# Sink attention and two MoE layers on one core: pinned weight conversions, one joint sink product, and two h groups moved in among the last attention steps

## Chip, cores and metric

The kernel runs on one core of one Trainium2 chip. The metric is the device time of one launch in microseconds (us); the figure used is the median of the runs.

## What is computed

Sliding-window attention with sink keys (2 batches, 8 heads, 768 positions, head dimension 64, 4 sinks, window 128), followed by two feed-forward layers of 1536 tokens, 512 -> 2048 -> 512, with two different activations.

```python
scores = scale * np.matmul(q, k.transpose(0, 1, 3, 2))
keep = is_sink | in_window          # first 4 keys, or the last 128
a = softmax(where(keep, scores, -1e9))
x = np.matmul(a, v)                 # to [1536, 512]
h = x @ w_in
g = where(h >= 1, h, where(h <= -1, 0, (h + 1) ** 2 / 4))
x = g @ w_out
h = x @ w2_in
out = (h * np.clip(h + 3.0, 0.0, 6.0) / 6.0) @ w2_out
```

The four weight matrices arrive as 64-bit floats. The kernel reads them as pairs of 32-bit words (a raw tile of 128 x 512 pairs, 512 KB) and makes 32-bit floats of them on the chip, and from these a high and a low part for the products.

## The kernel before

**Attention.** Two heads form a pair `j`; a pair belongs to one of four groups of query blocks (`GROUPS`, L28), four pairs to a group. Pairs 0 to 3 have four blocks of 128 queries each, pairs 4 to 7 two, pairs 8 to 11 two, pairs 12 to 15 four: 48 units in all. One unit (`j`, `u`) goes through these steps:

- `score` (L300): two fp32 products into `ps_s` (L310), on VectorE mask, scale and row maximum (L317); one step later `expo` (L336, ScalarE, with the row sums), one step later `normalise`: L328 and L329 on VectorE, then two multiplications of `p` on GpSimd (L331).
- `turn` (L357), three units later (`DIST`): TensorE transposes of `p` into `ps_t` (L371, L372) and a copy to `pt` (L353 on ScalarE or L355 on VectorE).
- `sinks` (L377), for units that also see the sinks beside their window: the four sink columns of each head are transposed into `ps_k` (L383, 4 x 128 each) and copied to `pts`.
- `mix` (L386), two steps after a pair's last `turn`: products of `pts` with the sinks' values `vs` and of `pt` with `vraw` into `ps_v` (L408), then `high` and `low` (L134, L136, L141) split the result into `xh` and `xl`.

The order of these steps on TensorE and on SyncE's DMA queue is the program's own (`manual_schedule`, L595). On VectorE, ScalarE and GpSimd the framework orders instructions by a timeline that it simulates while it builds the program: an instruction whose inputs it takes to be ready can come ahead of earlier ones. Each engine then runs its list strictly in order.

**Weights.** `load_w` (L158) loads a raw tile; there are four raw buffers (`RAW`), used in the order 0i0, 0o0, 0i1, 0o1, 0i2, ... (layer, in or out matrix, number). `take` starts a conversion, `narrow` (L168): absolute value (L174 VectorE or L176 ScalarE), clamp (L179), sign (L180), shift and merge (L181) on VectorE, the low word (L184) on ScalarE, and one step later the sum (L186) on VectorE, after which the raw buffer is free. Two steps later `split` makes the high part (L134 or L136) and the low part (L141). The first four raw tiles are loaded halfway through the attention's steps (L604), and 0i0, 0o0, 0i1 are taken 24, 14 and 6 steps before its end (L606 to L611).

**Layers.** For each `fc` (16 of them, a slice of 128 of the 2048 columns), `h_group(m, fc, c)` (L528) does 12 products of 512 columns for a chunk `c` of 512 tokens; `y_group` (L544) 12 more. For c = 0, `activate` follows at once (L511 to L513, then gh and gl by L134, L136, L141), for c = 1, 2 the result is put aside (`hs`, L134). The loop L624 to L636 runs h 0, y of the `fc` before, h 1, h 2 in each round. Tiles of `h` share four PSUM banks with `ps_s`.

## Time and profile before

| | us |
|---|---|
| median of 3 runs | 655.56 (654.04 to 656.28) |
| the profiled execution's own time | 655.16 |
| its span, first to last instruction | 653.40 |
| mean granted TensorE clock | 0.986 |
| TensorE busy | 630.7 (97%) |
| VectorE busy | 423.2 (65%) |
| ScalarE busy | 328.2 (50%) |
| GpSimd busy | 91.5 (14%, all of it in the first 117 us) |

The stages can be told apart by line: L310 to L408 are attention and end at 125.4 us, L534 and L564 are the layers. A busy share over the whole span hides the stages, so the rows further down are cut by stage. "Idle before" is the time an engine stood still before an instruction, and the name behind the arrow is what ended it.

### The profile page before, as it was taken

What the parts mean: (1) busy time and instruction counts of PE and PEld (TensorE: products, weight loads), DVE (VectorE), ACT (ScalarE), POOL (GpSimd) and SP (SyncE); (2) the same over time, 40 slices, a digit from 0 to 9 for tenths busy, and PEclk for the clock granted to TensorE, in tenths of its full rate; (3) what the DMA queues carried; (4) which work ended last, traced back from release to release, by engine and by line L of the source; (5) the groups of instructions that cost most, each with busy time, mean ns of one, the idle gap of its engine ahead of it and who ended that gap; (6) DMA issues with size and microseconds to landing.
All of it is one profiled execution on the core that took longest, in us unless ns stands there. A gap on an engine that the chain in (4) does not pass through costs nothing.

```text
span 653.4 us, 8514 instructions
## 1 busy us (share of the span) xinstructions
PE 630.7 (97%) x3008; PEld 493.6 (76%) x3008; DVE 423.2 (65%) x953; ACT 328.2 (50%) x669; POOL 91.5 (14%) x115
## 2 busy tenths in 40 slices
PE   7997797899999999999999999999999999999997
PEld 4554454588888887888888888888888888888886
DVE  4778888856647567539995597565668302994443
ACT  5777679655455445337663486455533223850001
POOL 7896687200000000000000000000000000000000
PEclk9999799899999999999999999999999999999999
DMA  4237257734453344102223575445451010523203
GB/s 129 88 115 247 70 167 233 229 107 141 129 161 129 115 144 128 65 32 97 98 96 118 174 236 182 162 129 161 129 158 68 34 64 1 192 98 96 97 32 130
DMA packets 32330, 81.38 MB, mean 125 GB/s; under 512 B 3056, under 2 KB 12320, under 8 KB 32288
## 3 DMA queue, kind: packets, MB, share of 16 engines
q1 hardware_dynamic: 32288, 80.84, 38.1%
q8 instruction: 24, 0.39, 0.3%
q14 instruction: 18, 0.15, 0.1%
HBM read 60.91 MB, written 19.92 MB: 124 GB/s over the span
## 4 chain that ended last, share of the span: by engine, by line
PE 72%; DVE 10%; DMA 9%; ACT 6%; issue 2%; POOL 1%; SPq 0%; ACTq 0%; POOLq 0%; DVEq 0%
PE ps_y L564 36%; PE ps_h L534 28%; DMA raw0o<-moe_w_out_dram 6%; PE ps_v L408 3%; PE ps_s L310 3%; DVE w L186 2%; DVE w L181 2%; DMA raw0i<-moe_w_in_dram 2%; ACT p L336 1%; PE ps_t L371 1%; ACT w L176 1%; ACT raw0o L184 1%; DVE w L179 1%; PE ps_t L372 1%; DVE r L512 1%
## 5 line engine op out<-in xcount | busy, mean ns | idle before, releaser
L534 PE MATMUL ps_h<-xh,wi 128*128 128x512 f32 x768 | 242.1, 390 | 0.0
L564 PE MATMUL ps_y<-gh,wo 128*128 128x512 f32 x768 | 241.6, 389 | 0.0
L534 PEld LDWEIGHTS ps_h<-xh,wi 128*128 128x128 f32 x768 | 144.5, 188 | 30.3 <-issue 0.3
L564 PEld LDWEIGHTS ps_y<-gh,wo 128*128 128x128 f32 x768 | 144.1, 188 | 29.9
L564 PE MATMUL ps_y<-gl,wo 128*128 128x512 f32 x384 | 149.6, 390 | 0.6 <-DVE gl L141 0.6
L534 PE MATMUL ps_h<-xl,wi 128*128 128x512 f32 x384 | 149.6, 390 | 0.0
L331 POOL TENSOR_SCALAR p<-p,sm 128x260 f32<-128x260 f32 (+2 forms) x96 | 88.1, 938 | 25.7 <-DVE sm L329 8.6
L564 PEld LDWEIGHTS ps_y<-gl,wo 128*128 128x128 f32 x384 | 72.1, 188 | 16.2 <-DVE gl L141 1.3
L534 PEld LDWEIGHTS ps_h<-xl,wi 128*128 128x128 f32 x384 | 72.2, 188 | 15.0
L179 DVE TENSOR_SCALAR w<-w 128x512 f32<-128x512 f32 x64 | 27.7, 433 | 43.9 <-ACT w L176 42.9
L134 ACT ACTIVATE hs<-ps_h 128x512 f32<-128x512 f32 x64 | 37.5, 589 | 36.4 <-PE ps_h L534 36.3
L336 ACT ACTIVATE p<-p,nm 128x260 f32<-128x260 f32 (+2 forms) x96 | 46.3, 483 | 15.0 <-DVE nm L317 11.4
L141 DVE TENSOR_TENSOR gl<-hs,gh 128x512 fp32r<-128x512 f32 x64 | 44.0, 688 | 12.7 <-ACT gh L134 11.9
L310 PE MATMUL ps_s<-kraw,qraw 64*128 64x260 f32 (+2 forms) x192 | 37.8, 469 | 7.8 <-DMA kraw<-k_dram 4.4
L512 DVE SCALAR_TENSOR_TENSOR r<-r 128x512 f32<-128x512 f32 x48 | 32.3, 685 | 15.6 <-ACT r L511 15.4
L141 DVE TENSOR_TENSOR wi<-w,wi 128x512 fp32r<-128x512 f32 x32 | 22.1, 690 | 30.6 <-ACT wi L134 29.6
L516 DVE SCALAR_TENSOR_TENSOR ps_h<-r,ps_h 128x512 f32<-128x512 f32 x16 | 11.1, 694 | 46.2 <-ACT r L515 46.2
L317 DVE CUSTOM_DVE_ANT_0 p<-ps_s,mask 128x260 f32<-128x260 f32 (+2 forms) x96 | 35.7, 396 | 7.7 <-PE ps_s L310 7.0
L134 ACT ACTIVATE gh<-ps_h 128x512 fp32r<-128x512 f32 x32 | 19.2, 598 | 33.6 <-DVE ps_h L513 21.7
L134 ACT ACTIVATE gh<-hs 128x512 fp32r<-128x512 f32 x35 | 22.0, 629 | 26.0 <-PE ps_y L564 24.8
L572 ACT ACTIVATE o<-ps_y 128x512 f32<-128x512 f32 x6 | 3.6, 596 | 62.5 <-PE ps_y L564 62.5
L136 DVE CAST gh<-hs 128x512 fp32r<-128x512 f32 x29 | 12.3, 426 | 32.8 <-PE ps_y L564 32.7
(72 smaller groups left out, 688.7 us busy)
## 6 DMA issues: line engine op xcount, KB each, us to landing
wo_d<-wo SPq DMA_DIRECT2D x32, 512.0 KB, 5.0
wo<-wo_d SPq DMA_DIRECT2D x32, 512.0 KB, 3.2
raw0i<-moe_w_in_dram SPq DMA_DIRECT2D x16, 512.0 KB, 3.4
raw0o<-moe_w_out_dram SPq DMA_DIRECT2D x16, 512.0 KB, 5.1
raw1i<-moe_w_in_dram SPq DMA_DIRECT2D x16, 512.0 KB, 3.4
raw1o<-moe_w_out_dram SPq DMA_DIRECT2D x16, 512.0 KB, 4.1
out_dram<-o SPq DMA_DIRECT2D x12, 256.0 KB, 2.2
qraw<-q_dram SPq DMA_DIRECT2D x8, 256.0 KB, 2.8
```

The lines of the kernel that those rows point to most:

```text
L134: nc.scalar.activation(out=dst, in_=src, func=AF.Copy)
L141: nc.vector.tensor_tensor(out=dst, in0=src, in1=f32(hi), op=ALU.subtract)
L179: nc.vector.tensor_scalar(out=f32(c), in0=f32(c), scalar1=F64_LOW, scalar2=F64_HIGH, op0=ALU.max, op1=ALU.min)
L181: nc.vector.scalar_tensor_tensor(out=c, in0=c, scalar=3, in1=hi, op0=ALU.logical_shift_left, op1=ALU.bitwise_xor)
L310: nc.tensor.matmul(banks[e], tq[rows, u * P:(u + 1) * P], tk[rows, c0:c0 + w], start=True, stop=True)
L317: nc.vector.tensor_tensor_reduce(out=p[:, e, :], in0=banks[e], in1=masks[min(i, 2)], scale=-SCALE, scalar=BIG, op0=ALU.add, op1=ALU.min, a ...
L331: nc.gpsimd.tensor_scalar_mul(out=p[:, e, :], in0=p[:, e, :], scalar1=sm[:, e:e + 1])
L336: nc.scalar.activation(out=p[:, e, :], in_=p[:, e, :], func=AF.Exp, scale=-1.0, bias=nm[:, e:e + 1], accum_out=sm[:, e:e + 1],)
L408: nc.tensor.matmul(ps[e * D:(e + 1) * D, u0 * P:u1 * P], l, r, start=n == 0, stop=n == len(ops[0]) - 1)
L512: nc.vector.scalar_tensor_tensor(out=r, in0=r, scalar=1.0, in1=r, op0=ALU.min, op1=ALU.mult)
L534: nc.tensor.matmul(ps, w[:, kc, :], x[:, kc, :], start=i == 0, stop=i == len(ops) - 1)
L564: nc.tensor.matmul(ys[dm], a[:, cs], b, start=fc == 0 and i == 0, stop=last and i == 2)
```

## The change

Four edits:

1. The instructions of `narrow` that read the raw tile are pinned behind everything already written for their engine, for the first layer's tiles 0 to 2 of each kind (`keep`).
2. Sinks: after `normalise`, for units with the wide row, a new VectorE instruction scales both heads' sink columns into a tile `psk` of 128 x 8. One transpose of `psk` replaces two of `p`, and one product with eight rows and 128 outputs replaces two with four rows and 64 outputs. `vs` becomes a block-diagonal tile of 8 x 128: GpSimd zeroes it and two DMAs fill it.
3. `h_group(0, 0, 0)` and `h_group(0, 0, 1)` are issued from the attention's steps, five and two steps before the last.
4. The tile that takes the second of these results lies in a pool of its own, opened before the attention.

```diff
+    hs0_p = ctx.enter_context(tc.tile_pool(name="hs0", bufs=1))
...
-    def narrow(t, dst):
+    def narrow(t, dst, keep):
+
+        def place(ins):
+            if keep:
+                tc.keep_in_program_order(ins)
...
-            nc.vector.tensor_scalar(out=c, in0=hi, scalar1=0x7FFFFFFF, scalar2=None, op0=ALU.bitwise_and)
+            place(nc.vector.tensor_scalar(out=c, in0=hi, scalar1=0x7FFFFFFF, scalar2=None, op0=ALU.bitwise_and))
         else:
-            nc.scalar.activation(out=f32(c), in_=f32(hi), func=AF.Abs)
+            place(nc.scalar.activation(out=f32(c), in_=f32(hi), func=AF.Abs))
...
-        nc.vector.tensor_scalar(out=hi, in0=hi, scalar1=-(1 << 31), scalar2=None, op0=ALU.bitwise_and)
+        place(nc.vector.tensor_scalar(out=hi, in0=hi, scalar1=-(1 << 31), scalar2=None, op0=ALU.bitwise_and))
...
-        nc.scalar.activation(out=f32(lo), in_=lo.bitcast(U32), func=AF.Copy, scale=2.0 ** -51, bias=2.0)
+        place(nc.scalar.activation(out=f32(lo), in_=lo.bitcast(U32), func=AF.Copy, scale=2.0 ** -51, bias=2.0))
...
-            narrow(t, t32)
+            narrow(t, t32, m == 0 and fc < 3)
...
-                ts = at_p.tile([NS, P], F32, tag="vs", name="vs")
-                nc.sync.dma_start(out=ts, in_=v[b, 0:NS, cs])
+                ts = at_p.tile([2 * NS, P], F32, tag="vs", name="vs")
+                nc.gpsimd.memset(ts, 0.0)
+                for e in range(2):
+                    ds = slice(e * D, (e + 1) * D)
+                    nc.sync.dma_start(out=ts[e * NS:(e + 1) * NS, ds], in_=v[b, 0:NS, cs][:, ds])
...
+                if w > 2 * P:
+                    ps = at_p.tile([P, 2, NS], F32, tag="psk", name="psk", bufs=DIST + 3)
+                    nc.vector.tensor_tensor(
+                        out=ps, in0=p[:, :, P:KB], in1=sm.unsqueeze(2).to_broadcast([P, 2, NS]), op=ALU.mult
+                    )
+                    psink[j, u] = ps.rearrange("p e s -> p (e s)")
                 for e in range(2):
                     nc.gpsimd.tensor_scalar_mul(out=p[:, e, :], in0=p[:, e, :], scalar1=sm[:, e:e + 1])
...
-                p = probs.pop((j, u))
-                for e in range(2):
-                    nc.tensor.transpose(ps[0:NS, e, n, :], p[:, e, P:KB], ident)
-            copy(pt[j][1][:, :, us[0]:us[-1] + 1, :], ps[0:NS, :, :len(us), :], 2 * len(us) * P)
+                nc.tensor.transpose(ps[0:2 * NS, n, :], psink.pop((j, u)), ident)
+            copy(pt[j][1][:, us[0]:us[-1] + 1, :], ps[0:2 * NS, :len(us), :], len(us) * P)
...
+            sink = us < nq
+            if sink:
+                nc.tensor.matmul(
+                    ps[:, us * P:nq * P], ts, tsink[:, us:nq, :].rearrange("p n q -> p (n q)"), start=True, stop=False
+                )
...
-                if us < nq:
-                    ops[e].append((us, nq, ts[:, cs], tsink[:, e].rearrange("p n q -> p (n q)")[:, us * P:nq * P]))
...
-            t = hs_p[0].tile([P, N], F32, tag=f"h{c}_{fc}", name=f"hs{c}")
+            t = (hs0_p if (c, fc) == (1, 0) else hs_p[0]).tile([P, N], F32, tag=f"h{c}_{fc}", name=f"hs{c}")
...
+                    if n == len(steps) - 5:
+                        h_group(0, 0, 0)
+                        early.append((0, 0, 0))
+                    if n == len(steps) - 2:
+                        h_group(0, 0, 1)
+                        early.append((0, 0, 1))
...
-                h_group(m, fc, 0)
+                if (m, fc, 0) not in early:
+                    h_group(m, fc, 0)
...
-                h_group(m, fc, 1)
+                if (m, fc, 1) not in early:
+                    h_group(m, fc, 1)
```

How the change moves instructions, at three places. In a row stand the line, the operation, what it writes `<-` what it reads (with the buffer's number), the shape of the output, and how often.

ScalarE before, while pairs 12 and 13 pass (L336 the exponentials of a unit, L353 the copies of transposes, L176, L184 and L134 a conversion):

```order
L353 ACTIVATE pts_1288<-ps_k_1341 4x2x256
L176 ACTIVATE w32_1682<-raw0i2_1394 128x512
L184 ACTIVATE raw0i2_1394<-raw0i2_1394 128x512
L336 ACTIVATE p_1351,sm_1353<-p_1351,nm_1352 128x260 x2
L353 ACTIVATE pt_1287<-ps_t_1388 128x2x256
L336 ACTIVATE p_1380,sm_1382<-p_1380,nm_1381 128x260
L353 ACTIVATE pts_1288<-ps_k_1401 4x2x256
```

ScalarE now, from the unit p_1395 of pair 14 on (L350 is the exponential, L367 the copy, L189 the low word, L135 the high part):

```order
L350 ACTIVATE p_1395,sm_1397<-p_1395,nm_1396 128x260 x2
L189 ACTIVATE raw0i0_943<-raw0i0_943 128x512
L367 ACTIVATE pt_1328<-ps_t_1434 128x2x256
L350 ACTIVATE p_1426,sm_1428<-p_1426,nm_1427 128x260
L367 ACTIVATE pts_1329<-ps_k_1449 8x256
L350 ACTIVATE p_1426,sm_1428<-p_1426,nm_1427 128x260
L350 ACTIVATE p_1457,sm_1459<-p_1457,nm_1458 128x260 x2
L367 ACTIVATE pt_1464<-ps_t_1466 128x2x256
L135 ACTIVATE wi0_1408<-w32_1409 128x512
```

Before, the conversion of the fifth raw tile (0i2) stood among the units of pair 13, and those of the first four far ahead of it; now the first raw tile (0i0) is converted there. Counted over ScalarE's list, 14 conversions stood ahead of the first layer's first activation before; now there are 3.

TensorE before, from the mix of pair 14 to the first h group (ps_t turns, ps_k sinks, ps_v mix, ps_h an h group):

```order
L408 MATMUL ps_v_1560<-pt_1418,vraw_1323 64x128 x2
...
L383 MATMUL ps_k_1589<-ident_114,p_1434 4x128 x2
L383 MATMUL ps_k_1589<-ident_114,p_1480 4x128 x2
L371 MATMUL ps_t_1596<-ident_114,p_1510 128x128
...
L383 MATMUL ps_k_1611<-ident_114,p_1540 4x128 x2
L408 MATMUL ps_v_1617<-pts_1549,vs_1456 64x512 x2
...
L534 MATMUL ps_h_1636<-xh0_0_363,wi0_1364 128x512
```

TensorE now:

```order
L421 MATMUL ps_v_1613<-pt_1464,vraw_1365 64x128 x2
...
L393 MATMUL ps_k_1641<-ident_117,psk_1511 8x128
L393 MATMUL ps_k_1641<-ident_117,psk_1553 8x128
L547 MATMUL ps_h_1645<-xh0_0_377,wi0_1408 128x512
...
L385 MATMUL ps_t_1667<-ident_117,p_1561 128x128
...
L547 MATMUL ps_h_1686<-xh0_1_803,wi0_1408 128x512
...
L405 MATMUL ps_v_1701<-pts_1600,vs_1503 128x512
...
L547 MATMUL ps_h_1735<-xh0_2_1371,wi0_1408 128x512
```

The h groups of chunks 0 and 1 now stand between the last turns, and the h group of chunk 2, which reads the result of the last mix, follows that mix directly.

ScalarE at the same place, before (p_1540 is the last unit, ps_v_1560 the mix of pair 14):

```order
L176 ACTIVATE w32_1824<-raw0o3_1703 128x512
L184 ACTIVATE raw0o3_1703<-raw0o3_1703 128x512
L336 ACTIVATE p_1540,sm_1542<-p_1540,nm_1541 128x260 x2
L184 ACTIVATE raw0i4_1705<-raw0i4_1705 128x512
L184 ACTIVATE raw0o4_1754<-raw0o4_1754 128x512
L176 ACTIVATE w32_1864<-raw0i4_1705 128x512
L134 ACTIVATE wi0_1775<-w32_1776 128x512
L134 ACTIVATE wo0_1823<-w32_1824 128x512
L134 ACTIVATE xh0_2_1327<-ps_v_1560 128x512
```

and now (ps_v_1701 is the last mix, L524 the activation of the h group that came early, gh its high part):

```order
L189 ACTIVATE raw0i1_947<-raw0i1_947 128x512
L367 ACTIVATE pts_1600<-ps_k_1641 8x256
L524 ACTIVATE r_1658<-ps_h_1645,half_116 128x512
...
L135 ACTIVATE wi0_1633<-w32_1634 128x512
L367 ACTIVATE pt_1599<-ps_t_1676 128x2x256
L367 ACTIVATE pts_1600<-ps_k_1682 8x256
L135 ACTIVATE gh_1659<-ps_h_1645 128x512
L189 ACTIVATE raw0i3_1673<-raw0i3_1673 128x512
L135 ACTIVATE hs1_1699<-ps_h_1686 128x512
L135 ACTIVATE xh0_2_1371<-ps_v_1701 128x512
```

Tile 0i3 is not among the pinned ones: its L189 stands ahead of the eviction of the last mix. On SyncE's queue its load keeps its place, and it takes the raw buffer that 0i1 leaves.

## Rows read from the trace of the kernel before

**Rows 1.** Engine busy by stage; columns after the stretch: its length, busy PE, PEld, DVE, ACT, POOL, granted clock, DMA.

```profile
59.77:84.20 24.43, 17.17 (x92) 9.06 (x90) 22.20 (x83) 17.06 (x53) 16.04 (x16) 0.79 0.41 139
84.20:92.87 8.67, 8.67 (x67) 4.97 (x65) 6.66 (x32) 7.47 (x25) 7.97 (x9) 1.00 0.59 192
92.87:101.96 9.09, 9.09 (x66) 5.25 (x65) 8.10 (x30) 8.10 (x24) 4.95 (x6) 1.00 0.32 99
101.96:114.93 12.97, 9.68 (x62) 5.00 (x61) 11.38 (x36) 11.98 (x31) 11.02 (x12) 0.92 0.89 302
114.93:125.36 10.43, 7.20 (x46) 4.33 (x44) 8.63 (x17) 7.84 (x15) 2.81 (x2) 0.83 0.85 234
125.36:653.40 528.04, 523.57 (x2306) 432.62 (x2304) 325.36 (x566) 234.80 (x394) 0.00 (x0) 1.00 0.36 117
```

**Rows 2.** TensorE's timeline, 60 to 126 us: start, length, idle before.

```profile
64.79 0.56 PE L310 MATMUL ps_s<-kraw,qraw 64*128 64x128 f32 x4 [3.37 <-DVE sm L328]
...
73.67 0.33 PE L371 MATMUL ps_t<-ident,p 128*128 128x128 f32 x1 [2.82 <-POOL p L331]
...
111.06 1.07 PE L408 MATMUL ps_v<-pts,vs 4*64 4x512 f32 x4 [2.44 <-ACT pts L353]
```

**Rows 3.** SyncE's queue: the first raw load and the key load behind four of them.

```profile
55.46 0.47 SPq L162 DMA_DIRECT2D raw0i<-moe_w_in_dram  x1
...
57.90 0.44 SPq L281 DMA_DIRECT2D kraw<-k_dram  x1
```

**Rows 4.** DMA issues, 57.8 to 58 us: that key load, us to landing.

```profile
kraw<-k_dram SPq DMA_DIRECT2D x1, 128.0 KB, 6.8
```

**Rows 5.** Engine busy, as rows 1, from the key load's landing on.

```profile
64.80:69.30 4.50, 4.50 (x22) 2.56 (x22) 4.35 (x14) 3.27 (x11) 2.41 (x2) 0.62 0.13 43
69.30:73.60 4.30, 1.56 (x13) 0.79 (x12) 4.30 (x18) 3.07 (x12) 0.90 (x2) 1.00 0.78 242
73.60:82.20 8.60, 7.45 (x31) 3.59 (x31) 6.70 (x25) 4.54 (x14) 8.24 (x10) 0.60 0.02 4
```

**Rows 6.** TensorE's timeline, pair 13: sinks, the next score, and a mix's two parts.

```profile
96.25 0.60 PE L383 MATMUL ps_k<-ident,p 128*4 128x128 f32 x4
96.78 0.71 PE L310 MATMUL ps_s<-kraw,qraw 64*128 64x260 f32 x4
...
99.07 1.07 PE L408 MATMUL ps_v<-pts,vs 4*64 4x512 f32 x4
100.08 1.95 PE L408 MATMUL ps_v<-pt,vraw 128*64 128x128 f32 x20
```

**Rows 7.** GpSimd's timeline: a memset, and eight multiplications in one run.

```profile
0.86 0.20 POOL L249 MEMSET mask<- 128x128 f32 x1
...
88.56 7.32 POOL L331 TENSOR_SCALAR p<-p,sm 128x260 f32<-128x260 f32 x8 [0.17 <-ACT p L336]
```

**Rows 8.** Groups by shape, attention: the nearest small VectorE instruction; columns busy us, mean ns.

```profile
L329 DVE RECIPROCAL sm<-sm 128x2 f32<-128x2 f32 x48 | 7.8, 162 | 1.0
```

**Rows 9.** The same view, VectorE, 125 to 246 us: two passes of a conversion, and the activation.

```profile
L179 DVE TENSOR_SCALAR w<-w 128x512 f32<-128x512 f32 x20 | 8.5, 427 | 22.6 <-ACT w L176 22.0
L512 DVE SCALAR_TENSOR_TENSOR r<-r 128x512 f32<-128x512 f32 x11 | 7.6, 688 | 5.1 <-ACT r L511 5.0
...
L186 DVE CUSTOM_DVE_ANT_0 w<-raw0o,w 128x1024 uint16<-128x1024 uint16 x10 | 6.9, 692 | 0.3
```

**Rows 10.** The chain that ended last, first layer: start and length of loads on it.

```profile
144.20 4.30 DMA raw0o<-moe_w_out_dram
...
190.51 4.22 DMA raw0o<-moe_w_out_dram
202.80 4.31 DMA raw0o<-moe_w_out_dram
...
236.87 4.08 DMA raw1o<-moe_w_out_dram
...
298.64 89.76 PE ps_y L564 x396
```

More of the change, by code (lines that the diff above doesn't have):

```diff
@@ L262, in build_fast_attention @@
             at[ci] = col0[-1] + nq * P
-        qk, vv, probs, pt = {}, {}, {}, {}
+        qk, vv, probs, psink, pt = {}, {}, {}, {}, {}
         def geom(gi):
@@ L362, in turn @@
                     at_p.tile([P, 2, NQ, 2, P], F32, tag="pt", name="pt", bufs=2),
-                    at_p.tile([NS, 2, NQ, P], F32, tag="pts", name="pts", bufs=2),
+                    at_p.tile([2 * NS, NQ, P], F32, tag="pts", name="pts", bufs=2),
                 )
-            p = probs[j, u]
+            p = probs.pop((j, u))
             w = widths[min(i, 2)]
@@ L373, in turn @@
             copy(pt[j][0][:, :, u, lo:, :], ps[:, :, lo:, :], 2 * (2 - lo) * P)
-            if i < 2:
-                probs.pop((j, u))
         def sinks(j, us):
-            ps = bank("ps_k").rearrange("p (e u q) -> p e u q", e=2, u=2)
+            ps = bank("ps_k").rearrange("p (u q) -> p u q", q=P)
             for n, u in enumerate(us):
-                p = probs.pop((j, u))
-                for e in range(2):
-                    nc.tensor.transpose(ps[0:NS, e, n, :], p[:, e, P:KB], ident)
-            copy(pt[j][1][:, :, us[0]:us[-1] + 1, :], ps[0:NS, :, :len(us), :], 2 * len(us) * P)
+                nc.tensor.transpose(ps[0:2 * NS, n, :], psink.pop((j, u)), ident)
+            copy(pt[j][1][:, us[0]:us[-1] + 1, :], ps[0:2 * NS, :len(us), :], len(us) * P)
         def mix(j):
@@ L408, in mix @@
                     nc.tensor.matmul(
-                        ps[e * D:(e + 1) * D, u0 * P:u1 * P], l, r, start=n == 0, stop=n == len(ops[0]) - 1
+                        ps[e * D:(e + 1) * D, u0 * P:u1 * P], l, r, start=n == 0 and not sink, stop=n == len(ops[0]) - 1
                     )
@@ L594, in sink_attention_moe_moe_kernel @@
     hs_p = []
+    early = []
     with tc.manual_schedule(engines={mybir.EngineType.PE, mybir.EngineType.SP}):
```

## The prediction

> **What bounds the kernel now.** I read the stages first [rows 1]. From 125.36 us on, the two layers are TensorE's: 523.57 of 528.04 us busy at full clock, and 396 products on the ending chain take 89.76 us [rows 10], 0.2267 us each, or 10.88 us for a round of 48. Nothing in the change removes a layer product, so what can be gained lies before 125.36 us. There the stretches cut at the ends of mixes 7, 11, 12, 13, 14 and 15 differ widely. While pair 12 passes, without a conversion beside it, TensorE is busy for all of 8.67 us and GpSimd for 7.97. Pairs 8 to 11, whose units are narrower, take 24.43 us with TensorE busy for 17.17, at a clock of 0.79. Pair 14 takes 12.97, busy for 9.68. The last turns and the last mix take 10.43, busy for 7.20 at 0.83.
>
> The idle gaps on TensorE [rows 2] name GpSimd's multiplications and ScalarE's copies. These are late because conversions stand in front of them on VectorE and ScalarE: VectorE is busy for 22.20 of the 24.43 us, against 6.66 of 8.67 beside pair 12. One gap is of another kind. The product at 64.79 is said to wait for VectorE, but it is the first score of pair 11, and that pair's keys were asked for at 57.90, behind four raw tiles asked for from 55.46 on [rows 3], and took 6.8 us [rows 4]: they land at 64.7. This wait is a transfer's, and the change leaves the order of those loads alone.
>
> **The sum.** The profiled execution took 655.16 us: 653.40 of span and 1.76 around it. That is 0.4 below the median of 655.56, and 0.3% (2 us) is about what a measurement of this kernel can tell from no change.
>
> *Sinks (A).* Four sink transposes take 0.53 us until the next score starts [rows 6]; two remain, 0.26 less in each of 16 calls: 4.2. Four sink records of 512 columns take 1.01 us until the mix goes on [rows 6]; two remain, 0.50 less in each of four mixes and half of that in the eight with 256 columns: 4.0. So TensorE has 8.2 us less to do. The copies to pts halve their columns, which I leave uncounted. Against it: 32 new small instructions on VectorE, each standing between the reciprocal and GpSimd, since GpSimd overwrites what they read. The trace has none; the nearest row is the reciprocal, 0.16 us [rows 8], together 5.2. And 12 memsets on GpSimd, at most 0.20 each by the wider one [rows 7], 2.4. GpSimd needs 7.32 us for a pair's eight multiplications without a pause [rows 7], so a pair of 8.67 us could not fall below some 7.5. The bounds are a gain of 8.2 (TensorE alone decides) and a loss of 7.6 (GpSimd alone decides and takes all additions). I take a gain of 4.5, a little over half, since beside pair 12 TensorE was the one without a pause and GpSimd had 8% left. The 12 extra DMAs for `vs` are of 1 KB, asked for two pairs ahead; SyncE's queue waits there for a buffer anyway, so I cost them at nothing; if that cover goes, the load behind them is the next pair's keys.
>
> *Conversions beside pairs 8 to 11 (B).* The orders show the first four conversions leave this stretch. After the keys' landing, from 64.80 to 82.20 us, TensorE is busy for 4.50 us at a clock of 0.62, 1.56 at 1.00 and 7.45 at 0.60 [rows 5]: 2.8 + 1.6 + 4.5 = 8.9 us of work at full speed in 17.4. The 3.37 us wait remains, and the low clock behind it, which cost 4.5 - 2.8 = 1.7. So 17.4 becomes 10.6 at best, a gain of 6.8; since three units' latency between score and turn may show where units are narrow, I take 6.0, with bounds of 3 and 6.8.
>
> *Pair 14 (C).* By ScalarE's order one conversion remains beside it, 0o0, and one (0i0) between pairs 13 and 14, where several stood. Beside pair 13 a conversion left the pair at 9.09 us. So 12.97 becomes 9.09, a gain of 3.9 (bounds 2 and 4.3, which is pair 12's 8.67).
>
> *The end (D).* Of the last 10.43 us, 7.20 at 0.83 are work, 6.0 at full speed. The waits for the last units' GpSimd and copies, 4.4 us with the clock's loss, get two h groups put into them, 2 x 12 x 0.2267 = 5.4 us, which the layers then do not have to do. They need xh of chunks 0 and 1, finished long before, and the weights of 0i0, converted some 20 steps earlier. I take all 4.4; the lower bound is 2, if the units' own chain to the last turn shows.
>
> *The first layer (E).* This is what the change pays with. Fourteen conversions stood ahead of the first activation, three do now, so in the first five rounds VectorE has to do about three a round, not two. One conversion is two passes like L179's 0.43 and three like L186's 0.69 [rows 9], 2.9 us; the activation's three passes, like L512's, are 2.1. Three conversions and one activation come to 10.8 us in a round of 10.88: it fits, with nothing over. And where before the h result of chunk 2 had two h groups between itself and the last mix, ScalarE now meets the low word of 0i3 ahead of that mix's eviction. That load starts when 0i1's sum is done. Mix 14's eviction (two passes) and 0i1's conversion follow mix 14 on VectorE, so that is some 4.3 us behind its end; with 4.3 to land [rows 10] ScalarE can go on some 8.7 us behind it, and the last mix ends at about 9.5. So the eviction is hardly late. I take a loss of 2.0 for both; the bounds are 0 and, from the load pace below, 10.5.
>
> Sum: 655.16 - 4.5 - 6.0 - 3.9 - 4.4 + 2.0 = **638.4 us**, rounded to 638, a gain of 17.
>
> **The rivals.**
>
> *GpSimd takes the sinks' gain.* For it: 92% busy beside pair 12 and a new instruction in front of it. Against: the additions are small. A becomes 0, the time 643. Chance 0.11.
>
> *The joint product saves nothing.* If the two heads' sink products ran side by side in the array, on different columns, one product would take as long as two. The row says otherwise: four records 1.01 us apart in all, 0.25 each, about the 0.21 that 512 columns take at 2.4 GHz, so one after the other [rows 6]. A falls by the mixes' half, to 2.3, the time to 641. Chance 0.04. The Trainium skill has the rule in "TensorE: Matmul & The Clock Gate", Part 3: Packing small matmuls: products with outputs on different column tiles run concurrently; by it the mixes would gain nothing. The trace does not agree here.
>
> *The layers lose their lead.* Before, loads of out tiles followed each other from 144.20 to 236.87 us eight times, 11.58 us apart [rows 10], slower than TensorE's 10.88; the lead in converted tiles hid it. Without that lead each of 15 rounds may cost 0.70: E becomes 10.5, the time 647. Against: a conversion's work fits the round, and early on loads are not what ScalarE's list is waiting for. Chance 0.17.
>
> *Slower.* The same place, worse: ScalarE stands in order behind each load, with gh and hs behind it, and every round takes as long as the longest gap, 190.51 to 202.80, 12.29 us [rows 10]. Fifteen rounds cost 21.2, the time 657.6. It decides from 12.2 us a round on, where 15 x 1.3 takes up the gains of 18.8. Against: the mean of the eight gaps is 11.58. Chance 0.04.
>
> *It only moves the waits.* ScalarE and VectorE may be just as late elsewhere, because the same conversions now crowd the last pairs; then B, C and D go and 653 remains at best. Only three of fourteen are left there. Chance 0.03.
>
> **How the numbers follow.** The forecast has the rest, 0.61. The range: all gains at their upper bounds and E at 0 give 655.2 - 8.2 - 6.8 - 4.3 - 4.4 = 631.5, and a keys' wait that shrinks from its 3.37 would take a little more: 629. Upward it takes in the first three rivals with a margin of some 3 us for gains that come short as well: 650. Faster by over 0.3%: 0.61 + 0.11 + 0.04 + 0.17 = 0.93; within it 0.03; slower 0.04.
>
> **What would show it.** Attention (scores, turns, mixes) ends with an h group between turns, and the last mix ends near 110 us, of which 5.4 are h groups; the gap of some 3 us in front of pair 11's first score stays, and the clock falls behind it. VectorE's busy share in pairs 8 to 11 falls clearly below 91%. Between the last two mixes TensorE has no gap over 1 us. Sink records in a mix: two, not four, in half the time. In the first layer, TensorE's gaps add up to about 2 us, named after gl, gh or wi. I am wrong if pairs 8 to 11 still take over 20 us, if GpSimd's pauses grow in pairs 12 to 15, or if gaps of the first layer sum to over 6 us.

## The result, and the profile after

| | before | after |
|---|---|---|
| median of the runs, us | 655.07 (654.04 to 656.28) | 639.95 (638.06 to 640.95) |
| the profiled execution's own time | 655.16 | 638.06 |
| its span | 653.40 | 636.30 |
| TensorE records | 3008 | 2952 |

The ratio is 0.9765, with a 95% interval of 0.9736 to 0.9795: faster, by some 15 us. The prediction was 638 in 629 to 650. So the total and the sign were right. Of the five terms behind them three were near, and two were wrong in opposite directions. A record is one entry of the profile; an fp32 product of the attention shows as two, a transpose as one. The profiled execution is the fastest of the four, with a mean granted clock of 1.000 where the other three had 0.990 to 0.994, so the rows below show some 2 us more gain than the medians.

Here is the windows view of the changed kernel, cut as [rows 1] at the ends of mixes 7, 11, 12, 13, 14 and 15. The columns are the same: length, busy PE, PEld, DVE, ACT, POOL, granted clock, DMA.

```profile
59.25:76.27 17.02, 12.57 (x93) 7.13 (x91) 10.33 (x56) 9.96 (x36) 11.45 (x14) 1.00 0.62 204
76.27:85.98 9.71, 8.96 (x60) 4.68 (x58) 7.95 (x41) 6.81 (x25) 9.23 (x11) 1.00 0.46 144
85.98:94.84 8.86, 8.67 (x60) 5.02 (x58) 7.92 (x37) 8.15 (x27) 5.42 (x7) 1.00 0.02 5
94.84:104.84 10.00, 8.51 (x56) 4.36 (x54) 9.18 (x33) 7.85 (x24) 9.54 (x12) 1.00 0.54 180
104.84:115.21 10.37, 10.37 (x65) 7.57 (x63) 6.30 (x10) 6.09 (x12) 2.83 (x3) 1.00 0.18 60
115.21:636.30 521.09, 517.11 (x2282) 427.85 (x2280) 339.78 (x601) 245.75 (x414) 0.00 (x0) 1.00 0.39 128
```

Beside [rows 1], stage by stage. The two early h groups (5.44 us of work) now lie in the last units; the fifth column takes them out there and puts them into the layers, so that like stands beside like.

| stretch | before | after | difference | with the h groups put back |
|---|---|---|---|---|
| start to mix 7 | 59.77 | 59.25 | -0.5 | -0.5 |
| pairs 8 to 11 | 24.43 | 17.02 | -7.4 | -7.4 |
| pair 12 | 8.67 | 9.71 | +1.0 | +1.0 |
| pair 13 | 9.09 | 8.86 | -0.2 | -0.2 |
| pair 14 | 12.97 | 10.00 | -3.0 | -3.0 |
| last turns, last mix | 10.43 | 10.37 | -0.1 | -5.5 |
| layers | 528.04 | 521.09 | -7.0 | -1.5 |
| span | 653.40 | 636.30 | -17.1 | -17.1 |

VectorE is busy for 10.33 of 17.02 us in pairs 8 to 11, 61% where it was 91%: the conversions have left. In pair 12 GpSimd is now the fullest engine, 9.23 of 9.71, while TensorE stands still for 0.75: that pair has become slower. GpSimd's own pauses did not grow there: from pair 12 to the last mix they sum to 4.4 us, where they were 6.8. Between the last two mixes TensorE has no pause.

TensorE's timeline of the changed kernel, five places: start, length, and in brackets the idle time before and what ended it.

```profile
64.03 0.49 PE L318 MATMUL ps_s<-kraw,qraw 64*128 64x128 f32 x4 [3.12 <-DMA kraw<-k_dram]
64.45 0.87 PE L421 MATMUL ps_v<-pt,vraw 128*64 128x256 f32 x8
...
82.41 0.71 PE L318 MATMUL ps_s<-kraw,qraw 64*128 64x260 f32 x4
83.05 1.12 PE L405 MATMUL ps_v<-pts,vs 8*128 8x512 f32 x2
84.10 1.95 PE L421 MATMUL ps_v<-pt,vraw 128*64 128x128 f32 x20
...
105.47 0.48 PE L547 MATMUL ps_h<-xh,wi 128*128 128x512 f32 x1
...
109.33 0.48 PE L547 MATMUL ps_h<-xh,wi 128*128 128x512 f32 x1
...
112.28 1.12 PE L405 MATMUL ps_v<-pts,vs 8*128 8x512 f32 x2
```

Three things are to be seen. The wait for pair 11's keys stayed, and the trace now names the transfer (before, it named VectorE, [rows 2]); but behind it the clock did not fall in this execution. The one sink product of pair 12 takes from 83.05 to 84.10, 1.05 us, for two records: the four before took 1.01 [rows 6], where the prediction wanted half the time. And the h groups stand at 105.5 and 109.3, among the last units.

### The profile page after: what moved, and what is told of

Its sections match the earlier page's. It is cut to its first block, busy times and chain, and to the rows that moved or that the text cites. A ratio compares the mean times of both kernels' runs of the same rounds, so it can differ in the third digit from the quotient of the medians.

```text
span 636.3 us, 8483 instructions
## 1 busy us (share of the span) xinstructions
PE 619.3 (97%) x2952; PEld 487.8 (77%) x2952; DVE 424.1 (67%) x985; ACT 324.5 (51%) x669; POOL 88.9 (14%) x127
## 4 chain that ended last, share of the span: by engine, by line
PE 89%; DVE 5%; ACT 3%; DMA 2%; issue 1%; POOL 1%; SPq 0%; DVEq 0%; ACTq 0%
PE ps_h L547 41%; PE ps_y L577 41%; ACT p L350 2%; PE ps_s L318 2%; PE ps_v L421 2%; DMA kraw<-k_dram 2%; DVE p L325 1%; PE ps_t L385 1%; PE ps_t L386 1%; PE ps_v L405 1%; POOL p L345 1%; DVE sm L336 1%; DVE pt L369 0%; DVE xl L142 0%; DVE sm L337 0%
## 5 line engine op out<-in xcount | busy, mean ns | idle before, releaser
L345 POOL TENSOR_SCALAR p<-p,sm 128x260 f32<-128x260 f32 (+2 forms) x96 | 83.8, 887 | 17.9 <-DVE sm L337 7.1
L350 ACT ACTIVATE p<-p,nm 128x260 f32<-128x260 f32 (+2 forms) x96 | 46.4, 484 | 27.4 <-DVE nm L325 19.4
L135 ACT ACTIVATE hs<-ps_h 128x512 f32<-128x512 f32 x64 | 37.5, 589 | 37.7 <-PE ps_h L547 36.0
L184 DVE TENSOR_SCALAR w<-w 128x512 f32<-128x512 f32 x64 | 27.4, 428 | 34.0 <-ACT w L181 33.4
L318 PE MATMUL ps_s<-kraw,qraw 64*128 64x260 f32 (+2 forms) x192 | 35.7, 447 | 7.5 <-DMA kraw<-k_dram 7.5
L525 DVE SCALAR_TENSOR_TENSOR r<-r 128x512 f32<-128x512 f32 x48 | 32.3, 686 | 12.3 <-ACT r L524 12.2
L135 ACT ACTIVATE gh<-hs 128x512 fp32r<-128x512 f32 x35 | 22.0, 630 | 25.9 <-PE ps_y L577 24.7
L135 ACT ACTIVATE gh<-ps_h 128x512 fp32r<-128x512 f32 x32 | 19.1, 597 | 25.2 <-DVE ps_h L526 12.9
```

The costliest lines, as they stand in the source:

```text
L135: nc.scalar.activation(out=dst, in_=src, func=AF.Copy)
L184: nc.vector.tensor_scalar(out=f32(c), in0=f32(c), scalar1=F64_LOW, scalar2=F64_HIGH, op0=ALU.max, op1=ALU.min)
L318: nc.tensor.matmul(banks[e], tq[rows, u * P:(u + 1) * P], tk[rows, c0:c0 + w], start=True, stop=True)
L345: nc.gpsimd.tensor_scalar_mul(out=p[:, e, :], in0=p[:, e, :], scalar1=sm[:, e:e + 1])
L350: nc.scalar.activation(out=p[:, e, :], in_=p[:, e, :], func=AF.Exp, scale=-1.0, bias=nm[:, e:e + 1], accum_out=sm[:, e:e + 1],)
L525: nc.vector.scalar_tensor_tensor(out=r, in0=r, scalar=1.0, in1=r, op0=ALU.min, op1=ALU.mult)
```

## The experiments

My theory after the result: the pins and the early h groups carry the gain, the first layer pays nothing, and the sinks edit nets to about nothing, because the two heads' products had run side by side and because GpSimd, not TensorE, sets the pace where the units are wide. The rivals are the terms as predicted, and those named in each expectation.

**1. The pins alone.** Edit 1 on the kernel before.

```diff
-            narrow(t, t32)
+            narrow(t, t32, m == 0 and fc < 3)
```

> The kernel before with the pinned conversion steps alone. My theory: pairs 8 to 11 give some 7 us and pair 14 some 3 by this edit alone, and the first layer loses nothing by the conversions that come to it: 655 - 10 = 645 us (643 to 647), pairs 8 to 11 (end of mix 7 to end of mix 11) in about 17 us. Rival 1, the layers lose their lead and only the two early h groups hid that: 648 or more, with gaps on TensorE in the first rounds. Rival 2, the pins only move the waits: 653 or more.

648.09 us (ratio 0.9900, 0.9879 to 0.9920), by the ratio a gain of 6.6 and not of 10 (in experiments 1 to 4 gains and losses against the kernel before go by the ratio). Windows of this kernel: pairs 8 to 11, 12, 14, and the end.

```profile
58.50:77.75 19.25, 16.57 (x92) 9.13 (x91) 11.03 (x54) 10.55 (x36) 12.09 (x15) 0.73 0.52 177
77.75:89.40 11.65, 10.38 (x66) 5.66 (x65) 7.24 (x35) 7.67 (x25) 10.54 (x13) 0.86 0.46 146
...
98.17:106.94 8.77, 8.42 (x63) 4.64 (x61) 7.77 (x29) 7.31 (x22) 7.25 (x8) 1.00 0.51 180
106.94:118.89 11.95, 8.64 (x47) 4.21 (x45) 4.18 (x6) 5.47 (x10) 3.92 (x5) 0.78 0.20 67
```

The mix of pair 12 on TensorE:

```profile
84.98 1.07 PE L412 MATMUL ps_v<-pts,vs 4*64 4x512 f32 x4 [1.27 <-DVE pts L359]
85.99 3.48 PE L412 MATMUL ps_v<-pt,vraw 128*64 128x128 f32 x20
```

Pairs 8 to 11 give 5.2 (24.43 to 19.25) and pair 14 gives 4.2 (12.97 to 8.77); the end takes 1.5 longer (11.95 where it took 10.43, at a clock of 0.78). But pair 12 goes from 8.67 to 11.65, with GpSimd busy for 10.54 of it. Of these 3.0 us, 1.3 are a wait of the mix for `pts`, copies of transposes of what GpSimd multiplied, and 1.5 are the clock: it fell in that mix, whose 20 records take 3.41 us until the pair ends at 89.40, where the kernel before took 1.89 (90.98 to 92.87). Over the two stretches together GpSimd has much the same to do (24.0 us before, 22.6 here): beside slow narrow pairs the multiplications of the wide units that follow were hidden; once those pairs are quick, they show (my reading; experiment 8 moves a part of them). The layers lost nothing: 527.51 us against 528.04, though here no h group runs early. So rival 1 of the expectation has its time, 648 or more, but not its reason: the layers did not lose their lead.

**2. The sinks edit alone.** Edit 2 on the kernel before.

> The kernel before with the sinks edit alone. My theory since the result: the joint product takes as long as the two it stands for, the transposes save about 0.2 us a call, and the small products on VectorE and GpSimd's memsets take that back: 654 to 656, no change. Rival 1, the term as predicted, 4.5 us: 650.6. Rival 2, GpSimd is held up behind the small products on VectorE: 657 or more, with GpSimd's waits for them over 3 us in all.

656.71 us (ratio 1.0033, 1.0018 to 1.0047): 2.2 us slower by the ratio, 1.1 by the medians. TensorE's waits by releaser, from mix 7 to 126 us, in this kernel (total, times, longest):

```profile
PE ps_v L400 <- ACT pts L362: 6.1, 3, 4.2
PE ps_s L313 <- DVE raw0o L180: 2.9, 1, 2.9
PE ps_t L380 <- POOL p L340: 1.0, 3, 0.5
```

The same view of the kernel before:

```profile
PE ps_v L408 <- ACT pts L353: 4.2, 2, 2.4
PE ps_t L371 <- POOL p L331: 4.2, 4, 2.8
```

The waits for GpSimd fall by 3.2 us, those for the copies of `pts`, which stand behind conversions on ScalarE, grow by 1.9. The predicted 4.5 us are not there. By stage the attention ends 1.2 us earlier (124.16 where it was 125.36), and the layers take 2.6 longer (530.64 where they took 528.04, with TensorE idle for 5.99 against 4.47), which none of the expectations named. Rival 2 has its sign, since GpSimd waits 4.2 us in all for `psk`, and 0.3 us are missing to its 657; but TensorE's waits for GpSimd became shorter, and those that grew are the copies'. So in this kernel rival 2 is neither shown nor excluded.

**3. The early h groups alone.** Edits 3 and 4 on the kernel before.

> The kernel before with the two early h groups alone (and the tile of their own that they need). My theory: the two groups (5.4 us) go into gaps of the last units, which are there with or without the pins: 655 - 4.5 = 650.6 (649 to 652). Rival, the gaps are there but VectorE and ScalarE, with the first conversions unpinned, put the groups' evictions in front of the last units' work: 653 to 656.

653.13 us (ratio 0.9962, 0.9944 to 0.9981), a gain of 2.5, between the gains of the two expectations (3 to 6 us, and 2 at most). Windows of pair 14, the end, and the layers:

```profile
100.52:114.43 13.91, 10.40 (x63) 5.46 (x61) 11.58 (x37) 12.47 (x32) 11.95 (x12) 0.88 0.86 295
114.43:125.18 10.75, 10.75 (x70) 7.80 (x68) 10.67 (x21) 9.32 (x18) 1.87 (x2) 1.00 0.66 196
125.18:649.80 524.62, 519.16 (x2282) 427.23 (x2280) 322.55 (x562) 232.00 (x390) 0.00 (x0) 1.00 0.36 118
```

Less their 5.44 the last units take 5.31 where they took 10.43: a gain of 5.1 in their place, by the mechanism of term D. Without the pins it is given back in part: pair 14 takes 13.91 (12.97 before), and the layers with the groups' 5.44 come to 530.06 (528.04 before), with TensorE idle for 5.46 there against 4.47.

**4. Pins and early h groups, without the sinks edit.**

> The changed kernel without the sinks edit: pins and early h groups. My theory: as fast as the changed kernel, 639 to 641, since the sinks edit is worth nothing. Rival 1, the sinks edit is worth the predicted 4.5: 644.5. Rival 2, it costs, by GpSimd's waits: 636 to 638, with pair 12 back at 8.7 us from 9.7.

642.00 us (ratio 0.9814, 0.9789 to 0.9839): 12.2 us less than before, where the pins alone and the h groups alone give 6.6 + 2.5 = 9.1. They help each other by some 3 us: the end, 11.95 with the pins alone, takes 10.75 with 5.44 of h groups in it. 642 lies between the expectations for the sinks edit's worth, so this kernel and the changed one ran once more, on the same chip:

> The changed kernel once more, on the same chip as the kernel without the sinks edit, for the difference of the two: 640 (639 to 641). Its clock behind the keys' wait should in most executions be below 1.00, unlike in the first profile.

> The kernel without the sinks edit once more, beside the changed kernel on the same chip. If the edit nets to about nothing, as with the raw tiles apart: within 1 us of the changed kernel. If it is worth what the first pair of runs showed: 642, 2 us above it.

640.84 with the sinks edit (ratio 0.9784, 0.9757 to 0.9810), 642.66 without (0.9818, 0.9787 to 0.9848): 1.8 us, near the second expectation, though the intervals overlap. The two profiled executions (640.82 and 644.54) differ by more: by 2.2 us in pairs 8 to 11, which use no sinks and where the granted clock was 0.90 with the edit and 0.74 without, by 1.9 in pair 12 (9.72 and 11.57), and by 1.3 the other way in pair 14 (9.99 and 8.74). The first profiles of the two kernels are alike in pairs 8 to 11 (17.02 and 16.90) and differ by 2.5 in pair 12 (9.71 and 12.23). So pair 12 is where the edit gains. TensorE and GpSimd there in the kernel without the edit:

```profile
86.59 1.07 PE L413 MATMUL ps_v<-pts,vs 4*64 4x512 f32 x4 [1.28 <-DVE pts L360]
87.59 3.38 PE L413 MATMUL ps_v<-pt,vraw 128*64 128x128 f32 x20
```

```profile
77.77 6.40 POOL L336 TENSOR_SCALAR p<-p,sm 128x260 f32<-128x260 f32 x7
84.35 3.67 POOL L336 TENSOR_SCALAR p<-p,sm 128x260 f32<-128x260 f32 x4 [0.17 <-DVE sm L334]
```

GpSimd multiplies for 10 us with one pause of 0.17, and the mix waits 1.28 us for `pts`, a copy of transposes of what GpSimd multiplied (1.27 in this kernel's first profile, and 1.27 with the pins alone). Behind the wait the clock fell here as in experiment 1 (0.87 over the pair, 1.00 with the edit): the mix's 20 records take 3.32 us until the pair ends at 90.91, those of the changed kernel 1.88 (84.10 to 85.98). With the edit the mix at 83.05 above has no wait: `psk` comes from VectorE, so the sinks no longer queue behind GpSimd. That this short cut, and the clock that it kept, is the edit's one real gain is my reading of these rows; no experiment isolates it, and the same wait does not always cost the clock: in experiment 7 without the edit the mix waits 1.34 us, and the clock of the pair is 1.00.

The changed kernel's second profile shows the clock behind the keys' wait as expected, below 1.00, and the mean clocks of all five executions are 0.991 to 0.997:

```profile
59.74:77.56 17.82, 13.97 (x92) 7.88 (x90) 10.42 (x56) 9.96 (x36) 11.45 (x14) 0.90 0.62 200
```

```profile
64.26 0.80 PE L318 MATMUL ps_s<-kraw,qraw 64*128 64x128 f32 x4 [2.86 <-DMA kraw<-k_dram]
64.99 1.55 PE L421 MATMUL ps_v<-pt,vraw 128*64 128x256 f32 x8
```

The same mix that took 0.87 us at 64.45 in the first profile takes 1.55 here, behind a wait of 2.86 us.

**5. The joint product as two of 64 columns.** The changed kernel with one product for each head, both on the 8 rows.

```diff
-                nc.tensor.matmul(
-                    ps[:, us * P:nq * P], ts, tsink[:, us:nq, :].rearrange("p n q -> p (n q)"), start=True, stop=False
-                )
+                for e in range(2):
+                    cs = slice(e * D, (e + 1) * D)
+                    nc.tensor.matmul(
+                        ps[cs, us * P:nq * P], ts[:, cs], tsink[:, us:nq, :].rearrange("p n q -> p (n q)"),
+                        start=True, stop=False,
+                    )
```

> The changed kernel, its one sink product of 128 output columns written as two of 64, one for each head, with the same right-hand side of 8 rows: four records a mix where there are two. If products on different output columns run side by side in the array (my theory now): the four records of pair 12 take the same 1.05 us until the mix goes on, and the time is that of the changed kernel, 639 to 641. If they run one after the other (what the prediction assumed): 2.1 us, 1.05 more in each of four mixes and some 0.6 in each of eight, up to 9 us more, 645 to 649.

640.65 us (ratio 0.9764, 0.9735 to 0.9793), the changed kernel's own ratio. TensorE's timeline, pair 12:

```profile
87.18 1.07 PE L407 MATMUL ps_v<-pts,vs 8*64 8x512 f32 x4
88.18 1.95 PE L424 MATMUL ps_v<-pt,vraw 128*64 128x128 f32 x20
```

Four records of 64 output columns take 1.00 us, two of 128 take 1.05. One after the other they would have taken 2.1. So the heads' products do run side by side, and joining them saves nothing. The single records say it too: of the four, two and two start 7 ns apart, here and in the kernel before (99.074 and 99.081, 99.554 and 99.561 us), while the two of the joint product start 0.53 us apart. That a record of fewer output columns is simply quicker does not fit: the transposes onto 4 columns [rows 6] and those onto 128 before them take 0.27 us each at full clock. By the Trainium skill ("TensorE: Matmul & The Clock Gate", Part 3: Packing small matmuls) products on different column tiles run concurrently; this run agrees, 1.00 us against 1.05, and the prediction's reading of the trace before was wrong.

**6. GpSimd leaves the sink columns alone.** The changed kernel; GpSimd multiplies two blocks of 128 columns, so that it need not wait for VectorE to read the four between them.

```diff
-            p = at_p.tile([P, 2, KB + P], F32, tag="p", name="p", bufs=DIST + 3)[:, :, :w]
+            pw = at_p.tile([P, 2, 2 * KB], F32, tag="p", name="p", bufs=DIST + 3)
+            p = pw[:, :, :w]
...
-                    nc.gpsimd.tensor_scalar_mul(out=p[:, e, :], in0=p[:, e, :], scalar1=sm[:, e:e + 1])
+                    x = p[:, e, :]
+                    if w > 2 * P:
+                        x = pw[:, e, :].rearrange("p (n c) -> p n c", c=KB)[:, :, 0:P]
+                    nc.gpsimd.tensor_scalar_mul(out=x, in0=x, scalar1=sm[:, e:e + 1])
```

> The changed kernel with GpSimd's multiplications leaving out the sink columns of p (two blocks of 128 columns, which nothing else needs the sink columns of), so that GpSimd no longer overwrites what VectorE's small product reads and need not wait for it. If that order is what the sinks edit costs: from the end of mix 0 to the end of mix 7 0.9 us less (40.08 to 39.2), pairs 12 and 14 together 2 us less: 637. If it is the small products' own time on VectorE, or GpSimd's multiplications: 639 to 641, with GpSimd as busy in pair 12 as before. Two blocks may also cost GpSimd more than one: 642 or more.

639.28 us (ratio 0.9750, 0.9726 to 0.9775): no change that can be told, the second expectation. GpSimd's waits, 19 to 106 us, first in the changed kernel, then here:

```profile
POOL p L345 <- DVE sm L337: 4.0, 5, 1.8
POOL p L345 <- DVE sm L336: 3.9, 2, 3.3
POOL p L345 <- DVE psk L340: 3.4, 7, 1.2
```

```profile
POOL p L349 <- DVE sm L338: 8.0, 8, 2.9
...
POOL p L349 <- DVE psk L341: 0.9, 1, 0.9
```

The wait for `psk` falls from 3.4 to 0.9 us and another takes its place. From the end of mix 0 to the end of mix 7 the 0.8 us that the first expectation wanted did come (40.08 to 39.29), though other kernels with the edit lie between 38.76 and 40.08 there; of its 2 us in pairs 12 and 14 only 0.2 came (19.71 to 19.52). So in the wide pairs at the end, standing behind VectorE's small product is not what costs GpSimd its time.

**7. The first raw tiles apart**, with and without the sinks edit. One raw tile every ten steps, so that the keys are not behind four of them.

```diff
-    def load_weights():
-        while issued[0] < min(taken[0] + RAW, len(queue)):
+    def load_weights(most=RAW):
+        end = issued[0] + most
+        while issued[0] < min(end, taken[0] + RAW, len(queue)):
...
-                    if n == len(steps) // 2:
-                        load_weights()
+                    if n - len(steps) // 2 in (0, 10, 20, 30):
+                        load_weights(1)
```

> The changed kernel with the first four raw weight tiles asked for one at a time, ten steps apart, and not all four ahead of pair 11's keys. If the keys' wait of 3.1 us is a transfer's that ends the line of work there: it shrinks below 1 us, pairs 8 to 11 take about 14 us and the time is 637. If GpSimd's multiplications are next: the wait goes, pairs 8 to 11 get shorter, pair 12 longer by as much, 639 to 641. If 0i0 comes late for its conversion: 642 or more.

> The same loads apart in the kernel without the sinks edit (pins and early h groups alone, 642.0). If the keys' wait ends the line of work: 639. If GpSimd's multiplications of the wide units are next, as pair 12's 12.23 us with GpSimd busy for 11.12 suggest: 641 to 643, and more so here, where TensorE has more to do beside it.

With the edit 637.97 us (ratio 0.9728, 0.9714 to 0.9743), without it 638.07 (0.9732, 0.9708 to 0.9755), where the first expectation was 639 and the second, GpSimd's, 641 to 643: there the keys' wait did set the time, and GpSimd did not take it back. Windows of pairs 8 to 11 and 12, with the edit:

```profile
59.64:72.44 12.80, 12.27 (x93) 7.08 (x91) 10.17 (x55) 9.86 (x36) 11.38 (x14) 1.00 0.80 254
72.44:84.41 11.97, 10.07 (x61) 5.60 (x59) 7.89 (x40) 6.76 (x25) 9.22 (x11) 0.86 0.55 177
```

TensorE's first wait in this stretch, with the edit:

```profile
64.57 0.71 PE L318 MATMUL ps_s<-kraw,qraw 64*128 64x260 f32 x4 [0.46 <-DMA kraw<-k_dram]
```

The wait for pair 11's keys is gone (the 0.46 us are for those of pair 12, whose scores are 260 columns wide), and pairs 8 to 11 take 12.80, less than expected. Pair 12 takes 11.97, 2.3 more, so the total came between the first two expectations: the time is lost again in the wide units behind. Half of the 2.3 is longer waiting (TensorE idle for 1.90 us, where it was 0.75), the other half the clock, 0.86 where it was 1.00 (busy for 10.07 us, where it was 8.96). And here the sinks edit is worth 0.1 us.

**8. A quarter of the wide multiplications on VectorE**, with the tiles apart, with and without the sinks edit.

```diff
-                    nc.gpsimd.tensor_scalar_mul(out=p[:, e, :], in0=p[:, e, :], scalar1=sm[:, e:e + 1])
+                    eng = nc.vector if e and u % 2 and w > 2 * P else nc.gpsimd
+                    eng.tensor_scalar_mul(out=p[:, e, :], in0=p[:, e, :], scalar1=sm[:, e:e + 1])
```

> The changed kernel with the raw tiles asked for apart, and one of every four of the wide units' multiplications (head two of every second unit) on VectorE and not on GpSimd. If GpSimd is what takes the sinks edit's gain and what pair 12 got back of the raw tiles' (both kernels with tiles apart: 638): pair 12 falls from 11.97 us to 10, pair 14 from 9.93 to 9.2, the pairs before by 0.5 in all: 634 to 635. If VectorE, busy for some 80% there, becomes late in its place: 638 or more.

> The same sharing without the sinks edit (pins, early h groups, raw tiles apart). Pair 12 falls from 11.52 us to 9.5; all other pairs are TensorE's: 636. So the sinks edit should be worth 1.5 to 2 us beside this one, the transposes' 0.17 us a call (pairs 5 to 7 took 12.00 to 12.33 with it against 12.58), where it is worth nothing without the sharing. If it is still nothing, GpSimd was not what held it up.

With the edit 634.78 us (ratio 0.9683, 0.9657 to 0.9708), without it 635.65 (0.9692, 0.9665 to 0.9720). Both totals came as expected, and both beat the changed kernel. Windows of pairs 12 to 14 with the edit:

```profile
72.13:84.03 11.90, 10.53 (x61) 5.79 (x59) 9.05 (x46) 7.20 (x26) 8.63 (x10) 0.86 0.57 188
84.03:92.30 8.27, 8.27 (x61) 4.73 (x59) 7.31 (x34) 7.62 (x24) 2.14 (x4) 1.00 0.00 0
92.30:101.28 8.98, 8.15 (x57) 4.41 (x55) 8.95 (x35) 7.61 (x22) 5.79 (x7) 1.00 0.49 155
```

The mix of pair 12 on TensorE, with the edit:

```profile
80.48 3.62 PE L422 MATMUL ps_v<-pt,vraw 128*64 128x128 f32 x20
```

Pair 12 without it:

```profile
71.19:81.28 10.09, 9.10 (x66) 5.04 (x64) 8.42 (x37) 7.51 (x26) 6.58 (x8) 1.00 0.69 222
```

Pair 14 falls from 9.93 to 8.98 and pair 13 from 8.86 to 8.27, where TensorE is busy throughout, below the 8.67 of a pair without the edit [rows 1]. Pair 12 falls by 1.4 without the edit (11.52 to 10.09), but hardly with it (11.97 to 11.90, clock 0.86 in both): that part of the expectation failed. The row above shows where: the mix's 20 records take 3.55 us until the pair ends at 84.03, where the changed kernel's took 1.88, so 1.7 us are the clock, and without them the pair would be at 10.2, near the 10 expected. What lowered the clock is open: TensorE's waits in that pair are 0.39, 0.51 and 0.48 us, those of the kernel without the edit 0.46 and 0.47, at a clock of 1.00. The edit should have been worth 1.5 to 2 us beside the sharing; the medians give 0.9, less than their intervals can tell from nothing.

## Why the prediction was right

**What bounds the kernel: right.** With the h groups put back, 15.6 of the 17.1 us came out of the stretch before the layers, and from 115.21 us on the profile names no wait of TensorE, which is busy for 517.11 of the 521.09 us.

**Term A, the sinks (-4.5): this step failed.** The net worth was measured beside four versions of the other edits:

| the rest of the kernel | without, us | with, us | difference |
|---|---|---|---|
| as before | 655.66 | 656.71 | +1.1 by medians, +2.2 by the ratio |
| pins and h groups (the change) | 642.66 | 640.84 | -1.8 |
| and raw tiles apart | 638.07 | 637.97 | -0.1 |
| and VectorE sharing | 635.65 | 634.78 | -0.9 |

Only the first difference is clear of its interval. So the gain that the prediction counted on is not shown anywhere; in the change the medians give 1.8 us. The mis-sized terms are these. The mixes' half, 4.0 us, is nothing (experiment 5); the rival with a chance of 0.04 was true. The prediction's sentence "the trace does not agree here" was a wrong reading: it compared 0.25 us a record with 0.21 for 512 columns at 2.4 GHz, which only the layers' products, of another type, come near (0.23 us each [rows 10]). The row to compare with stood in the same group: four transposes of 128 fp32 columns, 0.53 us [rows 6], 0.13 each, so 512 columns some 0.53 a record and four records 2.1 if they follow each other. The row had 1.01. Side by side was already in the trace before.

The transposes' half was 0.26 a call by the prediction; the two that are left take 0.31 us until the next score (86.48 to 86.79), so 0.22 less a call. But pairs 5 to 7, where TensorE hardly pauses, have three calls: they took 12.58 us before, 12.33 after and 12.00 in experiment 5, so 0.08 to 0.19 a call arrived, at most 3 us in sixteen. Even that arrives only where TensorE sets the pace. From the end of mix 0 to the end of mix 7, seven kernels without the edit take 39.14 or 39.15 us; the seven with it take from 38.76 to 40.08, six of them longer than without. Without it TensorE alone sets that stretch, with it no longer: in the changed kernel three mixes there wait 0.64, 0.80 and 0.19 us for the copies to `pts`, and without the edit none waits. The prediction left those copies uncounted.

On the other side stands what the prediction allowed for, VectorE's small products and GpSimd's memsets. Groups of the changed kernel, 19 to 106 us (count, busy us, mean ns):

```profile
L340 DVE TENSOR_TENSOR psk<-p,sm 128x8 f32<-128x8 f32 x29 | 5.5, 191 | 0.5
```

```profile
L345 POOL TENSOR_SCALAR p<-p,sm 128x260 f32<-128x260 f32 x58 | 54.1, 946 | 7.7 <-DVE sm L336 3.9 <-DVE psk L340 3.4 <-PE ps_v L421 0.3
...
L302 POOL MEMSET vs<- 8x128 f32 x10 | 2.0, 197 | 0.3 <-PE ps_v L405 0.2
```

0.19 us against the 0.16 taken from [rows 8], and 0.20 as taken from [rows 7]. The sizes were right; the gain was not.

**Term B, pairs 8 to 11 (-6.0): the size right, the account short.** The pins alone gave 5.2 there; the changed kernel 7.4 in the first profile and 6.6 in the second, whose clock in these pairs was 0.90. How the clock falls out moves this term by almost 3 us: the kernel of experiment 4 took 16.90 us there in one execution, at 0.90, and 20.01 in the other, at 0.74. The prediction's figure has the low clock in it, and the second profile is the case it described. What it missed is the next stretch: pair 12, which no term but A touched, is 1.0 us longer, and 3.0 with the pins alone (half of it the clock), because, as I read it, GpSimd's work for the wide units lost its cover. GpSimd was named as a bound for term A; that term B would run into it was not.

**Term C, pair 14 (-3.9): right in mechanism.** The pins alone give 4.2 (to 8.77); in the changed kernel 3.0 (to 10.00), with GpSimd at 9.54 of 10.00. The sinks edit takes 1.2 of it: the second kernel without it, beside the second run of the changed one, has 8.74 there.

**Term D, the end (-4.4): right.** 5.1 with the h groups alone, 5.5 in the changed kernel; "TensorE has no gap over 1 us" between the last two mixes was met. The last mix ended at 115.2 and not near 110: the gains ahead of it sum to 15.6 us and not to 18.8, which is the shortfall of A and C less what B and D gave beyond their sizes, and the 110 was 2 us short of the prediction's own sum (125.4 - 18.8 + 5.4 = 112).

**Term E, the first layer (+2.0): nothing was paid.** The work did move in. Windows of the changed kernel, its second and third round of 10.88 us from the last mix on:

```profile
126.09:136.97 10.88, 10.88 (x50) 9.01 (x49) 10.44 (x21) 7.48 (x13) 0.00 (x0) 1.00 0.69 230
136.97:147.85 10.88, 10.88 (x50) 9.01 (x49) 9.87 (x20) 8.23 (x16) 0.00 (x0) 1.00 0.68 216
```

VectorE is busy for 10.44 of 10.88 us, as close as the prediction's 10.8 ("it fits, with nothing over"), where it had 7.39 in the second round before; and TensorE has no gap at all. A full engine beside the bound cost nothing. With the h groups put back the layers came out 1.5 us shorter, of which the profile shows that the clock of the first round was 0.95 before and 1.00 now, and a last wait of 0.6 is gone; in the changed kernel's second profile they are 0.1 shorter. So the sum came right for a partly wrong reason, and that two misses of opposite sign nearly cancelled is luck. Against the first profile, with the start and pairs 12 and 13 put to A: A gave 4.8 less than forecast (+0.3 for -4.5) and C 0.9 less; E came out 3.5 better, B 1.4 and D 1.1. That leaves 0.3, the forecast gain of 16.8 against 17.1 in the profiled executions; by the ratio it is 15.4. Against the second profile, whose gain is 14.4, A gave 5.3 less and C 0.9 less; E came out 2.1 better, B 0.6 and D 1.1.

**The rivals.** "The joint product saves nothing" was true. "GpSimd takes the sinks' gain" was true in part: by the rows GpSimd is the fullest engine in pairs 12 and 14, where it also takes part of B and C, and a quarter of its wide multiplications on VectorE brought 3.2 us with the edit and 2.4 without. The lost lead, the slower rounds and waits that only move did not happen: experiment 1 has the pins without the h groups and its layers are no longer than before.

## What to carry to other kernels

Before two small products are joined, see whether they run side by side already: take the time of one record from a row with the same data type, and multiply. When a stretch is freed from work that slowed it, look at the stretch behind it, and ask which engine's queue was hidden by the slowness; here it was GpSimd's, and a quarter of its wide multiplications on VectorE, with the raw loads spread, brought 634.78 us, the best median (the same without the sinks edit, 635.65, cannot be told from it). When a stretch is longer than its waits explain, look at the granted clock before blaming an engine: in experiments 1 and 7 it was half of what pair 12 lost. An engine that becomes 96% busy beside the bound may still cost nothing, so price a crowded round by its waits and not by its busy share.

## What was not expected of the hardware

Two products on the two halves of the output columns share the array: four fp32 records of 512 columns in 1.00 us, in twos 7 ns apart, against 1.05 for two that use all columns.

The clock behind one and the same wait is not the same in every execution. Behind 3.12 us for pair 11's keys the granted clock of the stretch stayed at 1.00 in the changed kernel's first profile; behind 2.86 us in its second it was 0.90, and behind 4.32 us in experiment 5 it was 0.76. Pairs 8 to 11 took 17.02, 17.82 and 21.20 us, with the same work but for one pair's wait. And it fell where TensorE had hardly paused: in pair 12 of experiment 8 with the edit, after no wait longer than 0.51 us, the granted clock from the start of the mix to its end, 79.42 to 84.03 us, was 0.63.

A multiplication of 128 x 260 by a value for each row took 0.95 us on GpSimd; on VectorE it took less than half. Groups of experiment 8 with the sinks edit, 19 to 102 us:

```profile
L346 DVE TENSOR_SCALAR p<-p,sm 128x260 f32<-128x260 f32 x15 | 6.5, 431 | 0.4
```
